# Attention before a dense layer: q, k and v laid out by head pair on the host, the first batch alone, the second wholly between dense steps, weight tiles in 4 KB rows

## The chip, the cores and the metric

The kernel runs on one core of one Trainium2 chip. The metric is the time of one execution in device microseconds (us). One execution of the kernel before was taken with the hardware profiler; its rows stand below.

## The reference

Two batches, 8 heads, 576 positions, head dimension 64, fp32. Attention is the sum of two parts; then follow a dense mixture of 4 experts (every expert for every token) and a routed one of 8 experts (one expert for a token).

```python
q_d, k_d, v_d = (a.reshape(B, H, 144, 4, D).mean(axis=3) for a in (q, k, v))
out_up = np.repeat(softmax(q_d @ k_d.T / 8) @ v_d, 4, axis=2)
mask = np.abs(pos[:, None] - pos[None, :]) < 4
out_local = softmax(np.where(mask, q @ k.T / 8, -1e9)) @ v
x = (out_up + out_local).transpose(0, 2, 1, 3).reshape(1152, 512)
p = domain_probs / domain_probs.sum(-1)
x = sum(p[:, e:e+1] * (relu(x @ w1[e]) @ w2[e]) for e in range(4))
# then: cosine logits with 8 expert embeddings, best expert of each token, its gate * (relu(x @ w1b[e]) @ w2b[e])
```

## The kernel before

Attention works on 8 units; a unit is one pair of heads of one batch, its 2 x 64 dimensions on the 128 partitions. Units 0 to 3 are the first batch, 4 to 7 the second. For each unit q and k are loaded with positions on the partitions (`load_rows`, in runs of 256 bytes), transposed on TensorE (`turn`, `turn_k`, `turn_q`), copied out of PSUM (`keep_k`, `keep_q`) and pooled by fours (`pool_k`, `pool_q`, on POOL, GpSimd). v is loaded twice: by groups of four rows (`load_vg`) for the pooled part and by nine windows of 72 rows (`load_vw`) for the local part. Scores of the nine local blocks (`scores_a`, `scores_b`) and of the pooled part (`scores_d`) go to PSUM with the mask added by a matmul, then come maxima, exponentials, sums, scaling, transposes of P (`turn_pa`, `turn_pb`, `turn_pd`), copies out of PSUM (`keep_*`), products with v (`value_*`), the sum of both parts (`add_*`) and a split of x into a high and a low part (`hi`, `lo`), since the dense matmuls run as three products of such parts.

The order of all this is written out by hand. `ROUND` lists the 39 stages; in round i the stage with lag l works on unit i − l, so that up to six units are in flight. Every engine and every DMA queue runs its instructions in the order in which they are issued, and an instruction that waits holds up all behind it on its engine; all plain loads are issued on SP's queue. The attention runs alone until 36 pieces past the stage `lo` of unit 3. The 55 pieces left of 312 are then issued between the first 24 of 32 steps of the dense layer (line 582 on). A pair of steps is one `first_half` (12 matmuls of 256 columns) and one `second_half` (6 of 512 columns, of the pair before); 16 pairs cover the first two token chunks, that is 512 tokens of the first batch. The third chunk needs the second batch.

`Weights` loads tiles of 128 x 1024 fp32 (512 KB) into four raw tiles, splits each in two halves of a high and a low part (`halves`), and hands the raw tile back to load the next (`load_to`). A tile of w1 is loaded in runs of 1 KB, one of w2 in runs of 2 KB. When the second half of a tile is split, it loads ahead as far as raw tiles are there:

```python
if s == 1:
    self.raw.append(self.raws.pop(i))
    self.split += 1
    self.load_to(self.split + self.ahead)
```

Of the kernel before, what the change touches and what calls it, by code (L numbers as in the profile page):

```python
# [29 lines left out]
class Attention:  # L30
# [4 lines left out]
    ROUND = [  # L35
        ("value_a", 4), ("value_b", 4), ("value_d", 4), ("pool_v", 3), ("keep_q", 2), ("scores_a", 2), ("exp_b", 3),
        ("pool_k", 2), ("max_d", 3), ("sum_l", 3), ("scores_b", 2), ("lo", 5), ("max_a", 2), ("keep_d", 4),
        ("exp_d", 3), ("load_q", 1), ("pool_q", 2), ("exp_a", 2), ("scale_a", 3), ("scale_b", 3), ("sum_d", 3),
        ("scores_d", 2), ("turn_pa", 3), ("keep_pa", 3), ("load_vw", 2), ("scale_d", 3), ("add_a", 4), ("turn_pb", 3),
        ("add_b", 4), ("hi", 4), ("turn_pd", 3), ("turn_k", 1), ("turn_q", 1), ("load_k", 0), ("load_vg", 1),  # L40
        ("keep_pb", 3), ("keep_k", 1), ("keep_pd", 3), ("max_b", 2),
# [24 lines left out]
    def load_k(self, u, d):  # L66
        d["kn"] = self.load_rows(u, self.k, "kn")

    def load_q(self, u, d):
        d["qn"] = self.load_rows(u, self.q, "qn")  # L70

    def load_rows(self, u, src, tag):
        b, hp = self.units[u]
        t = self.ld.tile([96, 6, 2, D], F32, tag=tag, name=tag, bufs=2)
        for h in range(2):
            self.nc.sync.dma_start(out=t[:, :, h, :], in_=src[b, 2 * hp + h].rearrange("(j r) d -> j r d", r=6))
        return t

    def load_vg(self, u, d):
        nc, ld = self.nc, self.ld  # L80
        b, hp = self.units[u]
        vg = ld.tile([72, 2, 2, 4 * D], F32, tag="vg", name="vg", bufs=2)
        for h in range(2):
            nc.sync.dma_start(
                out=vg[:, :, h, :], in_=self.v[b, 2 * hp + h].rearrange("(a j r) d -> j a (r d)", a=2, r=4)
            )
        d["vg"] = vg

    def load_vw(self, u, d):
        nc, ld = self.nc, self.ld  # L90
        b, hp = self.units[u]
        vw = ld.tile([72, 9, 2, D], F32, tag="vw", name="vw", bufs=2)
        for h in range(2):
            off = ((b * H + 2 * hp + h) * S + 60) * D
            nc.sync.dma_start(
                out=vw[:, 1:8, h, :],
                in_=bass.AP(tensor=self.v.tensor, offset=off, ap=[[D, 72], [64 * D, 7], [1, D]]),
            )
        vs = self.v[b, 2 * hp:2 * hp + 2]
        nc.sync.dma_start(out=vw[0:68, 0], in_=vs[:, 0:68, :].rearrange("h p d -> p h d"))  # L100
        nc.sync.dma_start(out=vw[0:68, 8], in_=vs[:, 508:576, :].rearrange("h p d -> p h d"))
        d["vw"] = vw

    def turn(self, src, spots):
        ident = self.cst["ident"]
        for r, (t, o) in enumerate(spots):
            self.nc.tensor.transpose(t[:, o:o + 96], src[:, r].rearrange("p h d -> p (h d)"), ident[0:96, 0:96])

    def turn_k(self, u, d):
        d["tk"] = self.bank(), self.bank()  # L110
        self.turn(d["kn"], [(d["tk"][0], 96 * r) for r in range(5)] + [(d["tk"][1], 0)])

    def turn_q(self, u, d):
        d["tq"] = self.bank()
        self.turn(d["qn"], [(d["tk"][1], 96 + 96 * r) for r in range(4)] + [(d["tq"], 96 * r) for r in range(2)])

    def spread(self, T, t, o, r0, r1):
        src = t[:, o:o + 96 * (r1 - r0)].rearrange("p (r j) -> p r j", j=96)
        return T.rearrange("p (j r) -> p r j", r=6)[:, r0:r1, :], src

    def keep_k(self, u, d):
        kT = self.wk.tile([128, S], F32, tag="kT", name="kT", bufs=1)
        for t, o, r0, r1, e in ((d["tk"][0], 0, 0, 5, "a"), (d["tk"][1], 0, 5, 6, "a")):
            self.copy(e, *self.spread(kT, t, o, r0, r1))
        d["kT"] = kT

    def keep_q(self, u, d):
        qT = self.wk.tile([128, S], F32, tag="qT", name="qT", bufs=1)
        for t, o, r0, r1, e in ((d["tk"][1], 96, 0, 4, "a"), (d["tq"], 0, 4, 6, "v")):
            dst, src = self.spread(qT, t, o, r0, r1)  # L130
            if e == "a":
                self.nc.scalar.activation(out=dst, in_=src, func=AF.Copy, scale=0.125)
            else:
                self.nc.vector.tensor_scalar(out=dst, in0=src, scalar1=0.125, scalar2=None, op0=ALU.mult)
        d["qT"] = qT

    def fours(self, engine, T, out):

        e = self.nc.gpsimd if engine == "p" else self.nc.vector
        Tv = T.rearrange("p (g r) -> p g r", r=4)  # L140
        t = self.wk.tile([128, 144, 2], F32, tag="pt", name="pt")
        e.tensor_tensor(t, Tv[:, :, 0:2], Tv[:, :, 2:4], op=ALU.add)
        e.tensor_tensor(out, t[:, :, 0], t[:, :, 1], op=ALU.add)

    def pool_k(self, u, d):
        d["kd"] = self.cst["kd"][u % 2]
        self.fours("p", d["kT"], d["kd"][:, 0:144])

    def pool_q(self, u, d):
        d["qd"] = self.cst["qd"][u % 2]  # L150
        self.fours("p", d["qT"], d["qd"][:, 0:144])

    def pool_v(self, u, d):
        vg = d["vg"]
        e = self.nc.gpsimd if "p" == "p" else self.nc.vector
        t = self.wk.tile([72, 2, 2, 128], F32, tag="pv", name="pv")
        e.tensor_tensor(t, vg[:, :, :, 0:128], vg[:, :, :, 128:256], op=ALU.add)
        vd = self.wk.tile([72, 2, 2, D], F32, tag="vd", name="vd", bufs=2)
        e.tensor_tensor(vd, t[:, :, :, 0:64], t[:, :, :, 64:128], op=ALU.add)
        d["vd"] = vd  # L160
# [20 lines left out]
    def scores_a(self, u, d):  # L181
        self.scores(d, 0, 5)

    def scores_b(self, u, d):
        self.scores(d, 5, 9)
# [11 lines left out]

    def max_a(self, u, d):
        d["mx"] = self.wk.tile([128, 9], F32, tag="mx", name="mx", bufs=2)
        self.nc.vector.tensor_reduce(out=d["mx"][:, 0:5], in_=d["s0"], axis=AX.X, op=ALU.max, negate=True)  # L200

    def max_b(self, u, d):
        self.nc.vector.tensor_reduce(out=d["mx"][:, 5:9], in_=d["s5"], axis=AX.X, op=ALU.max, negate=True)

    def max_d(self, u, d):
        m = self.wk.tile([128, 3], F32, tag="mxd", name="mxd", bufs=2)
        self.nc.vector.tensor_reduce(out=m, in_=d["sd"], axis=AX.X, op=ALU.max, negate=True)
        self.nc.vector.tensor_scalar(out=m, in0=m, scalar1=1.0 / 16, scalar2=None, op0=ALU.mult)
        d["mxd"] = m

    def exp(self, P, src, bias, sm, scale=1.0):
# [4 lines left out]
    def exp_a(self, u, d):  # L216
        d["P"] = self.wk.tile([128, 9, 72], F32, tag="P", name="P", bufs=2)
        d["sm"] = self.wk.tile([128, 9], F32, tag="sm", name="sm", bufs=2)
        for i in range(5):
            sm = d["sm"][:, i:i + 1] if i < 5 else None  # L220
            self.exp(d["P"][:, i], d["s0"][:, i], d["mx"][:, i:i + 1], sm)

    def exp_b(self, u, d):
        for i in range(5, 9):
            sm = d["sm"][:, i:i + 1] if i < 5 else None
            self.exp(d["P"][:, i], d["s5"][:, i - 5], d["mx"][:, i:i + 1], sm)

    def exp_d(self, u, d):
        d["Pd"] = self.wk.tile([128, 3, 144], F32, tag="Pd", name="Pd", bufs=2)
        d["smd"] = self.wk.tile([128, 3], F32, tag="smd", name="smd", bufs=2)  # L230
        for i in range(3):
            sm = d["smd"][:, i:i + 1] if i < 3 else None
            self.exp(d["Pd"][:, i], d["sd"][:, i], d["mxd"][:, i:i + 1], sm, 1.0 / 16)

    def weights(self, P, sm, known, weight):

        if known < sm.shape[1]:
            self.nc.vector.tensor_reduce(out=sm[:, known:], in_=P[:, known:], axis=AX.X, op=ALU.add)
        self.nc.vector.tensor_scalar(out=sm, in0=sm, scalar1=1e-9, scalar2=weight, op0=ALU.add, op1=ALU.mult)
        self.nc.vector.reciprocal(sm, sm)  # L240
        return sm

    def sum_l(self, u, d):
        d["rc"] = self.weights(d["P"], d["sm"], 5, 1.0)

    def sum_d(self, u, d):
        d["rcd"] = self.weights(d["Pd"], d["smd"], 3, 4.0)

    def scale(self, engine, P, rc):
        e = self.nc.gpsimd if engine == "p" else self.nc.vector  # L250
        e.tensor_tensor(P, P, rc.unsqueeze(2).to_broadcast(list(P.shape)), op=ALU.mult)

    def scale_a(self, u, d):
        self.scale("p", d["P"][:, 0:4], d["rc"][:, 0:4])
# [1034 lines left out]
```

## Time and profile before

| | us |
|---|---|
| median of 3 runs (lowest, highest) | 696.08 (694.25, 696.15) |
| the profiled execution, its own time | 692.35 |
| its span, first to last instruction | 690.6 |
| TensorE (PE) busy | 653.1 (95%) |
| VectorE (DVE), ScalarE (ACT), GpSimd (POOL) busy | 345.9, 261.0, 144.6 |
| mean granted TensorE clock | 0.989 |

Times in rows are us from the first instruction; PEld is the weight load of TensorE, which overlaps its matmuls. "Idle before" names what ended an engine's idle time. The granted clock is a share of the full 2.4 GHz.

### The profile page before, as it was taken

The numbers are of one execution on the slowest core, as the hardware profiler recorded it, in microseconds if no ns is written. First come the engines' busy times: TensorE is split into PE (matmuls) and PEld (weight loads), VectorE is DVE, ScalarE is ACT, GpSimd is POOL, SyncE is SP. The second block draws the span as 40 slices with busy tenths as digits, with TensorE's granted clock in tenths as the row PEclk, the third lists the DMA queues.
The fourth block names the chain that finished last, engine by engine and source line by source line (L and its number), as shares of the span: only waits on it lengthen the run. The fifth ranks groups of instructions, "written<-read, shape, count | busy, mean of one in ns | idle before, by whom it ended". The sixth has DMA issues, their size and how long they took to land. (4 is left out here: it accounts for less than half of the span.)

```text
span 690.6 us, 11440 instructions
## 1 busy us (share of the span) xinstructions
PE 653.1 (95%) x4287; PEld 578.2 (84%) x4287; DVE 345.9 (50%) x825; ACT 261.0 (38%) x653; POOL 144.6 (21%) x203
## 2 busy tenths in 40 slices
PE   5798999999999999999999999999799998999896
PEld 4677899989999999999999999999698877788675
DVE  2667764213444122342132326989662269489751
ACT  3577742112232111231111222243342367488642
POOL 4678511100000000000000001748441122121111
PEclk9799999999999999999999999999999999999999
DMA  8866250000331002031001126251672166499600
GB/s 219 207 146 147 57 162 3 1 1 31 93 121 62 1 0 62 1 125 58 1 30 62 54 68 187 62 184 64 181 240 78 32 211 204 151 333 349 222 20 29
DMA packets 78364, 73.57 MB, mean 107 GB/s; under 512 B 32286, under 2 KB 62254, under 8 KB 78272
## 3 DMA queue, kind: packets, MB, share of 16 engines
q1 hardware_dynamic: 75968, 66.09, 31.6%
q0 software_dynamic: 2304, 6.33, 3.1%
q8 instruction: 48, 0.79, 0.5%
q14 instruction: 44, 0.36, 0.2%
HBM read 66.10 MB, written 7.09 MB: 106 GB/s over the span
## 5 line engine op out<-in xcount | busy, mean ns | idle before, releaser
L529 PE MATMUL psb<-wh,hT 128*128 128x512 f32 x576 | 197.6, 395 | 0.0
L520 DVE SCALAR_TENSOR_TENSOR hT<-psb,hT 128x384 fp32r<-128x384 f32 (+1 forms) x104 | 54.7, 526 | 221.2 <-ACT hT L519 221.1
L519 ACT ACTIVATE hT<-psb 128x384 fp32r<-128x384 f32 (+1 forms) x104 | 48.6, 467 | 290.2 <-PE psb L515 290.1
L515 PE MATMUL psb<-xh,wh 128*128 128x384 f32 (+1 forms) x416 | 135.5, 326 | 0.0
L515 PE MATMUL psb<-xl,wh 128*128 128x384 f32 (+1 forms) x416 | 134.9, 324 | 0.0
L515 PE MATMUL psb<-xh,wl 128*128 128x384 f32 (+1 forms) x416 | 134.9, 324 | 0.0
L529 PEld LDWEIGHTS psb<-wh,hT 128*128 128x128 f32 x576 | 108.6, 189 | 20.6 <-issue 0.4
L529 PE MATMUL psb<-wl,hT 128*128 128x512 f32 x288 | 113.4, 394 | 0.0
L403 POOL TENSOR_TENSOR wl<-raw,wh 128x512 fp32r<-128x512 f32 x24 | 31.8, 1358 | 306.2 <-DVE waste L752 290.4
L515 PEld LDWEIGHTS psb<-xh,wh 128*128 128x128 f32 x416 | 78.2, 188 | 4.3
L515 PEld LDWEIGHTS psb<-xl,wh 128*128 128x128 f32 x416 | 78.3, 188 | 4.1
L515 PEld LDWEIGHTS psb<-xh,wl 128*128 128x128 f32 x416 | 78.2, 188 | 0.0
L403 DVE TENSOR_TENSOR wl<-raw,wh 128x512 fp32r<-128x512 f32 x108 | 71.9, 712 | 4.5 <-ACT wh L399 3.7
L399 ACT CAST wh<-raw 128x512 fp32r<-128x512 f32 x126 | 70.8, 624 | 0.1
L529 PEld LDWEIGHTS psb<-wl,hT 128*128 128x128 f32 x288 | 54.3, 189 | 7.8
L1064 PE MATMUL psb<-wh,gx 128*128 128x256 f32 x288 | 58.2, 289 | 0.1
L1032 PE MATMUL psb<-wh,hT 128*128 128x512 f32 x160 | 54.2, 399 | 1.6 <-ACT sqd L1042 0.8
L1064 PEld LDWEIGHTS psb<-wh,gx 128*128 128x128 f32 x288 | 46.2, 189 | 1.9 <-issue 1.2
L1032 PEld LDWEIGHTS psb<-wh,hT 128*128 128x128 f32 x160 | 30.1, 188 | 7.8 <-ACT sqd L1042 1.2
L1064 PE MATMUL psb<-wl,gx 128*128 128x256 f32 x144 | 35.9, 283 | 0.0
L1032 PE MATMUL psb<-wl,hT 128*128 128x512 f32 x80 | 31.5, 394 | 0.0
L1064 PEld LDWEIGHTS psb<-wl,gx 128*128 128x128 f32 x144 | 27.2, 189 | 0.4
(250 smaller groups left out, 849.8 us busy)
## 6 DMA issues: line engine op xcount, KB each, us to landing
raw<-in_moe_w_dram SPq DMA_DIRECT2D x66, 512.0 KB
late_raw<-in_moe_w_dram SPq DMA_DIRECT2D x20, 512.0 KB
acc<-in_moe_w_dram SPq DMA_DIRECT2D x10, 512.0 KB
kn<-in_k_dram SPq DMA_DIRECT2D x16, 144.0 KB
qn<-in_q_dram SPq DMA_DIRECT2D x16, 144.0 KB
vg<-in_v_dram SPq DMA_DIRECT2D x16, 144.0 KB
rows<-acc SPq DMA_DIRECT2D x9, 256.0 KB
vw<-in_v_dram SPq DMA_DIRECT2D x16, 126.0 KB
```

The costliest lines, as they stand in the source:

```text
L399: nc.scalar.copy(hi[:, c], t[:, c])
L403: lo_eng.tensor_tensor(lo[:, c], t[:, c], hi[:, c].bitcast(F32), op=ALU.subtract)
L515: nc.tensor.matmul(t, a[:, kk, fs], b_[:, kk, xs], start=(n == 0), stop=(n == 11))
L519: nc.scalar.activation(out=hi, in_=t, func=AF.Relu)
L520: nc.vector.scalar_tensor_tensor(out=lo, in0=t, scalar=0.0, in1=hi.bitcast(F32), op0=ALU.max, op1=ALU.subtract)
L529: nc.tensor.matmul(ys[t], a[:, ts], b_[:, f % 2, :], start=(f == 0 and j == 0), stop=(f == 7 and j == 2))
L1032: nc.tensor.matmul(y, gh[:, f, a], b_[:, f % 2, :], start=(n == 0), stop=(n == 23))
L1064: nc.tensor.matmul(dst, a[:, kk], w[:, kk, :], start=(n == 0), stop=(n == 11))
```

## The change

The host lays out q and k as they are needed on chip, one array of 128 partitions (two heads x 64 dimensions) x 576 positions for a unit, and v as 72 rows that hold the nine windows (1152 numbers) and the groups of four (1024 numbers) of two heads. The transposes of q and k and the copies behind them go away, and with them the factor 0.125 on q; it is now in the exponentials' scale and in a scaling of the maxima (`top`). A unit has four loads instead of ten. q is pooled on DVE by one reduce, k on POOL as before. The local blocks are parted 4 and 5, not 5 and 4; two copies (`od`, half of `dT`) move from DVE to ACT; sums are inverted in two parts (`sum_a`, `sum_b`). The weights are stored so that each tile is one array of 128 rows of 4 KB. `run` takes an order and a range of units: `ALONE` for the first batch, with one weight half after each `exp_b`, `BESIDE` for the second, its 144 pieces spread over the first 28 of the 32 dense steps. No stage of the second batch is issued ahead of the first dense step.

```diff
+    ALONE = [
+        ("load_qk", 0), ("max_a", 1), ("sum_a", 2), ("scale_a", 2), ("value_d", 4), ("keep_d", 4), ("pool_v", 2),
+        ("turn_pa", 3), ("exp_d", 2), ("sum_b", 2), ("turn_pd", 3), ("value_b", 4), ("scores_a", 0), ("sum_d", 2),
+        ("add_a", 4), ("turn_pb", 3), ("add_b", 4), ("keep_pa", 3), ("keep_db", 3), ("pool_q", 0), ("pool_k", 0),
+        ("scores_b", 0), ("exp_a", 1), ("keep_8", 3), ("value_a", 3), ("scale_b", 2), ("keep_da", 3), ("scale_d", 2),
+        ("max_b", 1), ("max_d", 1), ("hi", 4), ("keep_pb", 3), ("scores_d", 0), ("lo", 4), ("exp_b", 1), ("load_v", 1),
+    ]
+    BESIDE = [
+        ("keep_pb", 4), ("scores_b", 2), ("max_b", 2), ("pool_k", 1), ("scores_a", 1), ("pool_v", 3), ("exp_a", 2),
+        ("sum_a", 2), ("exp_b", 2), ("scores_d", 2), ("max_d", 2), ("value_a", 4), ("value_d", 4), ("sum_b", 2),
+        ("load_v", 2), ("keep_d", 4), ("turn_pa", 3), ("value_b", 4), ("exp_d", 2), ("add_a", 4), ("keep_pa", 3),
+        ("scale_d", 3), ("turn_pd", 3), ("keep_da", 3), ("add_b", 4), ("load_qk", 0), ("scale_a", 2), ("keep_db", 3),
+        ("sum_d", 2), ("keep_8", 3), ("hi", 4), ("scale_b", 2), ("pool_q", 1), ("lo", 4), ("turn_pb", 3), ("max_a", 1),
+    ]
...
+    def run(self, order, units):
+        for i in range(len(units) + max(lag for _, lag in order)):
+            for name, lag in order:
+                if 0 <= i - lag < len(units):
+                    u = units[i - lag]
                     getattr(self, name)(u, self.st.setdefault(u, {}))
                     yield name, u
...
+    def load_qk(self, u, d):
+        b, hp = self.units[u]
+        t = self.ld.tile([128, 2, S], F32, tag="qk", name="qk", bufs=3)
+        self.nc.sync.dma_start(out=t[:, 1, :], in_=self.k[b, hp])
+        self.nc.sync.dma_start(out=t[:, 0, :], in_=self.q[b, hp])
+        d["qT"], d["kT"] = t[:, 0, :], t[:, 1, :]
+    def load_v(self, u, d):
         b, hp = self.units[u]
+        vg = self.ld.tile([72, 2, 2, 4 * D], F32, tag="vg", name="vg", bufs=2)
+        self.nc.sync.dma_start(out=vg.rearrange("p a h d -> p (a h d)"), in_=self.v[b, hp, :, 1152:])
+        vw = self.ld.tile([72, 9, 2, D], F32, tag="vw", name="vw", bufs=3)
+        self.nc.sync.dma_start(out=vw.rearrange("p i h d -> p (i h d)"), in_=self.v[b, hp, :, 0:1152])
+        d["vg"], d["vw"] = vg, vw
...
     def pool_q(self, u, d):
         d["qd"] = self.cst["qd"][u % 2]
-        self.fours("p", d["qT"], d["qd"][:, 0:144])
+        self.nc.vector.tensor_reduce(
+            out=d["qd"][:, 0:144], in_=d["qT"].rearrange("p (g r) -> p g r", r=4), axis=AX.X, op=ALU.add
+        )
...
+    def top(self, m, s, scale):
+        self.nc.vector.tensor_reduce(out=m, in_=s, axis=AX.X, op=ALU.max)
+        self.nc.vector.tensor_scalar(out=m, in0=m, scalar1=-scale, scalar2=None, op0=ALU.mult)
...
+            self.nc.sync.dma_start(out=t, in_=w[c])
...
+        half = H // 2
+        for name, u in att.run(att.ALONE, range(half)):
+            if name == "load_v" and u < 2:
+                W.load_to(u + 1)
+            elif name == "load_v" and u == 3:
                 W.load_to(NRAW)
+            elif name == "exp_b":
+                W.halves(1, "a", "v")
...
-        W.halves(max(0, 4 - W.half), "v", "v")
-        rest, done = pieces - first, 0
+        run = att.run(att.BESIDE, range(half, 2 * half))
+        rest, done = half * len(att.BESIDE), 0
         for step in range(32):
...
-            while done < min(rest, -(-rest * (step + 1) // 24)):
+            while done < min(rest, -(-rest * (step + 1) // 28)):
                 next(run)
                 done += 1
             if W.half < 2 * n_a:
```

## Rows read from the trace of the kernel before

**Rows 1.** Busy us of each engine in a stretch; then granted clock, DMA share, GB/s.

```profile
49.09:57.65 8.56, 7.58 (x124) 6.10 (x122) 6.82 (x17) 6.69 (x29) 6.84 (x10) 1.00 0.60 145
...
80.00:100.00 20.00, 20.00 (x170) 17.79 (x169) 13.81 (x28) 11.30 (x35) 3.95 (x3) 1.00 0.62 175
```

**Rows 2.** Timeline of PE: start us, us, line, output<-inputs, shape, count.

```profile
5.05 1.19 PE L107 MATMUL psb<-ident,kn 96*128 96x96 f32 x6 [5.05 <-DMA kn<-in_k_dram]
...
27.84 2.19 PE L319 MATMUL psb<-acc,vw 68*64 68x64 f32 x36
...
38.80 1.27 PE L319 MATMUL psb<-acc,vw 68*64 68x64 f32 x36
...
75.81 0.39 PE L515 MATMUL psb<-xh,wh 128*128 128x256 f32 x1
...
98.35 0.40 PE L529 MATMUL psb<-wh,hT 128*128 128x512 f32 x1
...
101.13 0.39 PE L529 MATMUL psb<-wh,hT 128*128 128x512 f32 x1
...
128.41 0.34 PE L515 MATMUL psb<-xh,wh 128*128 128x384 f32 x1
```

**Rows 3.** Timeline of PE: a steady round's scores; values of a unit beside dense.

```profile
49.09 0.32 PE L165 MATMUL psb<-mask,dup 64*128 64x360 bf16 x1
...
50.12 0.29 PE L165 MATMUL psb<-mask,dup 64*128 64x288 bf16 x1
...
50.89 0.90 PE L192 MATMUL psb<-kd,qd 64*64 64x144 f32 x12
...
93.69 1.27 PE L319 MATMUL psb<-acc,vw 68*64 68x64 f32 x36
...
95.43 0.50 PE L529 MATMUL psb<-wh,hT 128*128 128x512 f32 x1
```

**Rows 4.** Groups of 0 to 80 us: busy us, mean ns | idle before.

```profile
L403 DVE TENSOR_TENSOR wl<-raw,wh 128x512 fp32r<-128x512 f32 x5 | 4.6, 921 | 0.1
...
L200 DVE TENSOR_REDUCE mx<-psb 128x5 f32<-128x360 f32 x8 | 4.2, 523 | 3.9 <-PE psb L175 3.9
...
L134 DVE TENSOR_SCALAR qT<-psb 128x192 f32<-128x192 f32 x8 | 4.0, 504 | 11.0 <-PE psb L107 11.0
...
L64 DVE COPY dT<-psb 72x288 f32<-72x288 f32 x6 | 2.7, 450 | 0.2
...
L208 DVE TENSOR_SCALAR mxd<-mxd 128x3 f32<-128x3 f32 x7 | 2.6, 366 | 0.2
...
L64 DVE COPY od<-psb 128x144 f32<-128x144 f32 x6 | 1.8, 300 | 0.0
...
L240 DVE RECIPROCAL sm<-sm 128x9 f32<-128x9 f32 x7 | 1.5, 216 | 0.2
```

**Rows 5.** Two stretches of 2 us, columns as in rows 1.

```profile
4.00:6.00 2.00, 0.95 (x6) 0.93 (x6) 0.00 (x0) 0.00 (x0) 0.00 (x0) 1.00 0.92 158
12.00:14.00 2.00, 2.00 (x26) 1.72 (x22) 0.55 (x2) 1.51 (x10) 1.52 (x2) 1.00 1.06 360
```

**Rows 6.** Timeline around a q load: SP's issues and PE's wait.

```profile
20.23 0.39 SPq L375 DMA_DIRECT2D raw<-in_moe_w_dram  x1
...
20.72 1.25 SPq L76 DMA_DIRECT2D qn<-in_q_dram  x2
...
26.69 1.22 PE L107 MATMUL psb<-ident,qn 96*128 96x96 f32 x6 [1.83 <-DMA qn<-in_q_dram]
```

**Rows 7.** The last part, columns as in rows 1.

```profile
610.00:650.00 40.00, 35.29 (x229) 30.79 (x228) 34.08 (x69) 31.05 (x65) 6.08 (x6) 1.00 0.98 327
```

**Rows 8.** Stretches around a fall and rise of PE's clock, columns as in rows 1.

```profile
20.00:26.00 6.00, 3.09 (x28) 2.11 (x23) 5.43 (x11) 3.42 (x15) 4.87 (x5) 1.00 0.81 209
28.00:36.00 8.00, 8.00 (x96) 6.47 (x97) 3.85 (x12) 4.35 (x22) 5.53 (x8) 0.50 1.01 233
38.00:40.00 2.00, 2.00 (x49) 1.89 (x49) 1.75 (x6) 1.61 (x4) 0.33 (x1) 1.00 0.66 148
```

More of the change, by code (lines that the diff above doesn't have):

```diff
@@ L79, in load_vg @@
-    def load_vg(self, u, d):
-        nc, ld = self.nc, self.ld
-        b, hp = self.units[u]
[L82 to L135, printed above, removed]
@@ L231, in exp_d, with inverse, sum_a, sum_b @@
         for i in range(3):
[L232 to L238, printed above, removed]
+            self.exp(d["Pd"][:, i], d["sd"][:, i], d["mxd"][:, i:i + 1], d["smd"][:, i:i + 1], 0.125 / 16)
+    def inverse(self, sm, weight):
         self.nc.vector.tensor_scalar(out=sm, in0=sm, scalar1=1e-9, scalar2=weight, op0=ALU.add, op1=ALU.mult)
         self.nc.vector.reciprocal(sm, sm)
-        return sm
-    def sum_l(self, u, d):
-        d["rc"] = self.weights(d["P"], d["sm"], 5, 1.0)
+    def sum_a(self, u, d):
+        self.inverse(d["sm"][:, 0:4], 1.0)
+    def sum_b(self, u, d):
+        self.nc.vector.tensor_reduce(out=d["sm"][:, 4:9], in_=d["P"][:, 4:9], axis=AX.X, op=ALU.add)
+        self.inverse(d["sm"][:, 4:9], 1.0)
     def sum_d(self, u, d):
[L247 to L251, printed above, removed]
+        self.inverse(d["smd"], 4.0)
+    def scale(self, P, rc):
+        self.nc.gpsimd.tensor_tensor(P, P, rc.unsqueeze(2).to_broadcast(list(P.shape)), op=ALU.mult)
     def scale_a(self, u, d):
-        self.scale("p", d["P"][:, 0:4], d["rc"][:, 0:4])
+        self.scale(d["P"][:, 0:4], d["sm"][:, 0:4])
     def scale_b(self, u, d):
-        self.scale("p", d["P"][:, 4:9], d["rc"][:, 4:9])
+        self.scale(d["P"][:, 4:9], d["sm"][:, 4:9])
     def scale_d(self, u, d):
-        self.scale("p", d["Pd"], d["rcd"])
+        self.scale(d["Pd"], d["smd"])
     def turn_p(self, d, t, o, i):
@@ L324, in value_a @@
     def value_a(self, u, d):
-        self.values(d, 0, 5)
+        self.values(d, 0, 4)
     def value_b(self, u, d):
-        self.values(d, 5, 9)
+        self.values(d, 4, 9)
     def add(self, d, b0, b1):
         n = 64 * (b1 - b0)
+        if "x" not in d:
+            d["x"] = self.wk.tile([128, S], F32, tag="x", name="x")
         self.nc.vector.tensor_tensor(
@@ L563 @@
         nc.gpsimd.dma_start(out=pr, in_=probs.rearrange("(t p) e -> p t e", p=128))
-        pieces = len(att.units) * len(att.ROUND)
-        run = att.run()
-        first = 0
-        for n, (name, u) in enumerate(run, 1):
-            if n == 14:
-                W.load_to(NRAW)
-            if n >= 20 and (n - 20) % 8 == 0 and W.half < 4:
-                W.halves(1, "v", "v")
-            if name == "lo" and u == H // 2 - 1:
-                first = n + 36
-            if n == first:
-                break
+        half = H // 2
[3 more added lines that the diff above has]
+            elif name == "load_v" and u == 3:
+                W.load_to(NRAW)
+            elif name == "exp_b":
+                W.halves(1, "a", "v")
         nc.vector.tensor_reduce(out=psm, in_=pr, axis=AX.X, op=ALU.add)
@@ L1261, with laid @@
 _OUTS = [((N, DM), "float32")]
+def laid(np, name, a):
+    if name in ("q", "k"):
+        return a.reshape(B, H // 2, 2, S, D).transpose(0, 1, 2, 4, 3).reshape(B, H // 2, 128, S)
+    if name == "v":
+        w = np.zeros((B, H // 2, 72, 9, 2, D), a.dtype)
+        for i in range(9):
+            c0, c1 = max(64 * i - 4, 0), min(64 * i + 68, S)
+            w[:, :, 0:c1 - c0, i] = a[:, :, c0:c1].reshape(B, H // 2, 2, c1 - c0, D).transpose(0, 1, 3, 2, 4)
+        g = a.reshape(B, H // 2, 2, 2, 72, 4 * D).transpose(0, 1, 4, 3, 2, 5)
+        return np.concatenate([w.reshape(B, H // 2, 72, -1), g.reshape(B, H // 2, 72, -1)], axis=3)
+    if name.endswith("_w1"):
+        return a.reshape(-1, 4, 128, 4, 256).transpose(0, 3, 2, 1, 4).reshape(-1, 4, 128, 1024)
+    if name.endswith("_w2"):
+        return a.reshape(-1, 4, 2, 128, DM).transpose(0, 1, 3, 2, 4).reshape(-1, 4, 128, 1024)
+    return a
 def kernel(**inputs):
```

104 lines of the change are left out of this document (34 added, 70 removed).

## Prediction, made before the result was known

> **What bounds the kernel now.** I read the page's totals first, then the busy time by stretch, the matrix unit's timeline, the groups of instructions of the first 80 us, and last the load queue. By stretch there are two regimes [rows 1]. From 80 us on TensorE (PE) is full, with no idle time left in 80 to 100, so every microsecond of PE work added or removed there counts whole. Before 80 us no engine is full: in a steady round of the attention (one unit, that is one head pair of one batch, passes each stage once) PE has 7.58 of 8.56 us, DVE 6.82, ACT 6.69 and POOL 6.84. The first dense matmul starts at 75.81, and its third token chunk, the first that needs the second batch, at 128.41 [rows 2]. What comes behind 128.41 is the same work in both kernels. So the forecast is a sum of two terms: how much earlier dense work starts, and how much more attention PE then carries between dense steps.
>
> **Dense side: what attention costs there.** A pair of dense steps (one call of each half) takes 101.13 − 98.35 = 2.78 us [rows 2]. Ahead of 128.41 stand 16 first halves and 15 second ones, 15.5 pairs, 43.1 us. The stretch took 128.41 − 75.81 = 52.6, so attention took 9.5 us of PE between the steps. That was the score blocks 5 to 8 and the pooled scores of the last unit, and all transposes of P and value products of the last two (55 pieces of the hand-written order were left). Scores of one unit, from a steady round: 50.89 − 49.09 = 1.80 us for the local blocks and 0.90 for the pooled ones, 2.7; the part named is 50.89 − 50.12 + 0.90 = 1.67 [rows 3]. So turns and values cost (9.5 − 1.67) / 2 = 3.9 us a unit, seams with the dense work included; directly, the values alone are 95.43 − 93.69 = 1.74 [rows 3]. After the change four whole units lie there: 4 × (2.7 + 3.9 + 0.2 for more seams) = 27.2 us, which is 17.7 more. The PSUM banks get tighter: at the change of chunk four are held for dense sums, and a unit's pieces want up to six. The trace has no row for such a wait; below it costs nothing (DVE is busy 13.81 and ACT 11.30 of 20 us in 80 to 100, with attention and weight halves beside the dense work, so they can keep up [rows 1]), above perhaps one dense pair, 2.8. I take 1.1, nearer to the covered end. Together +18.8.
>
> **Alone side: when dense starts.** Gone per unit are 12 transposes of q and k on PE, three copies out of PSUM on ACT, one on DVE and the two POOL adds that pool q; of loads, ten strided issues become four. DVE becomes the busiest engine: 6.82 a unit now, less 0.50 (q), 0.45 (half of dT) and 0.30 (od), which go or move to ACT, plus a reduce of q over 576 elements (0.52 for 360, so about 0.8), four more operations on a few columns (two scalings behind the maxima, a second addition and reciprocal of the sums; 0.22 for a reciprocal now, 0.37 for a scaling, 0.8 in all, as most are like the first) and one low half of a weight tile (0.92) [rows 4]: 8.1 us. Four units are 32.4. The first score block can start where the first transposes do now, 5.05 us [rows 2], and takes about 1.5; the last unit's copies, products and adds that DVE waits for are some 3. Nothing else waiting, dense starts at 5.05 + 1.5 + 32.4 + 3 = 42 us. That is the lower end.
>
> Two waits speak against it. They come from the order of SP's queue. Every second weight half frees a raw tile and at once loads ahead as far as there are tiles: four weight tiles, the last of which has to wait until DVE has split the first one, the last DVE instruction of round 2. Behind that waiting load on SP stand v of unit 1 and q, k of unit 3. DVE gets there at about 5.05 + 1.5 + 10 us of work and some gaps, say 18. Then 0.52 + 0.63 + 0.59 MB have to move: at the best rate of the trace, 360 GB/s [rows 5], 4.9 us, plus issue and flight. Now a q load issued at 20.72, right behind such a weight load, is used at 26.69, and PE idles for it [rows 6]. So q, k of unit 3 are there at about 25, while PE has done its 3 units of scores and unit 0's first turns by 19.5: it waits 5.5 us, with unit 0's other turns and values queued behind, and DVE's pooling of q with two maxima behind it. The second: the next reload waits for DVE's end of round 4, v of unit 3 stands behind it, and POOL's sum of v stands ahead of the two scalings that the last turns need. 0.82 MB are 2.3 us, about 2 of flight, less about 1 that POOL has left to do: 3.5 us. With 1 us for a low clock I take 42 + 5.5 + 3.5 + 1 = 52 us. The upper end is the last rival's.
>
> The rule behind these waits is in the Trainium skill, "DMA: Bandwidth & Descriptors", section "Anatomy of one DMA": DMA engines do not wait on semaphores, the issuing sequencer does, before dispatch. By that rule everything behind the reload is late as above, and the start is 52; were it not so, it would be 42. The row agrees so far as a load behind a reload was late there.
>
> **Sum.** −(75.8 − 52) + 18.8 = −5.0 us. The profiled execution took 692.35 (span 690.6 and 1.75 around it), so it would be 687.3 like for like; the median of the runs shown, 696.08, lies 3.7 above that execution, and the forecast for it is **691.1 us**.
>
> **Weights in 4 KB rows.** The loads were 1 KB or 2 KB runs. In the dense part nobody waits for weights, so I cost them at nothing there; the cover is PE's full queue. In 610 to 650 the DMA share is near 1, and DVE, which splits, is busy 34.1 of 40 us [rows 7]. No wait there is put down to a weight load.
>
> **Rivals.**
> *The loads do not hold (23%).* The reload is ready earlier than I place it, or the large rows move faster; for it speaks that rows of 2.3 to 4.6 KB replace runs of 256 bytes, which held the DMA at share 0.92 with only 158 GB/s [rows 5]. Dense starts at 42: −33.8 + 18.8 = −15.0, 681.1 us.
>
> *The clock stays low (30%), the one on the other side.* PE's granted clock was 1.00 in 20 to 26, where PE was busy 3.1 of 6 us, then 0.50 in 28 to 36, where it was full, and 1.00 again from 38 [rows 8]. In that stretch a round (values of one unit to those of the next) took 38.80 − 27.84 = 10.96 instead of 8.56 [rows 1, 2]. The waits above leave PE as idle as there, and the drain of four units has no fifth to fill it; two units of the pipeline hardly overlap. If each of four rounds costs the 2.4 us more, the start goes from 52 to 61.6: −14.2 + 18.8 = +4.6, 700.7 us. It decides from a dense start later than 75.8 − 18.8 = 57. Against it: the first dense work is dense enough to raise the clock again. The Trainium skill, "TensorE: Matmul & The Clock Gate", Part 1, has the throttled state as the default, released by activity; by it the alone stage with less PE work for the same latency is the place to lose the clock, and the time goes towards 700.7. The rows just named agree.
>
> *The rows pay in the tail (5%).* If what looks like DVE's pace in 610 to 650 were hidden load time, its 5.9 idle us could go: 691.1 − 5.9 = 685.2. Against it: no wait on these tiles is listed.
>
> **Numbers.** Forecast 42%, then 23, 30 and 5. A measurement of this kernel tells about 0.3%, 2.1 us, from no change: faster is under 694.0, slower over 698.2. Of the 42, 32 lie under 694.0 (a start up to 55 us) and 10 within; of the clock's 30, 23 lie over 698.2 and 7 within. Faster 0.32 + 0.23 + 0.05 = 0.60, same 0.17, slower 0.23. The forecast's own range is 686 to 696 (start 47 to 57); for 8 in 10 it reaches to the loads that hold nothing up, 679, and to the low clock, 700.
>
> **What would show it.** The first dense matmul at about 52 us; third chunk some 71 us later (43.1 + 27.2 + 1.1). PE idle before the scores of unit 3 with a load of q or k as releaser, and before the last turns of P with POOL as releaser, itself held by v. Granted clock 0.50 somewhere in 20 to 52. No transposes from q and k, no ACT copies of them. Behind the third chunk the same length as before. Wrong would be: a start at 42 without those waits; PE idle between the dense steps for banks or for DVE by more than 3 us; a tail that changes.

## The result, and the profile after

The changed kernel took **705.23 us** (median of 4 runs, 703.41 to 706.0), the kernel before 695.5 in the same comparison (694.25 to 696.15): ratio 1.0139, 95% interval 1.0121 to 1.0157. It is slower, and 14.1 us over the forecast of 691.1, outside the range of 679 to 700. The profiled execution took 703.41 with a span of 701.7.

The timeline of the matrix unit in the changed kernel, for the rows of [rows 2] that start the dense work and its third chunk:

```profile
58.23 0.58 PE L462 MATMUL psb<-xh,wh 128*128 128x256 f32 x1
...
136.15 0.34 PE L462 MATMUL psb<-xh,wh 128*128 128x384 f32 x1
```

Dense work starts 17.58 us earlier than before (75.81), but the third chunk comes 77.92 us behind it, where it was 52.60: 25.32 more. So at the third chunk the kernel is 7.74 us behind. From there to the end of the span it needs 565.6 us, against 562.2 before: another 3.4 us.

Busy time by stretch, of the stage before dense work and of the stretch from the first dense matmul to the third chunk (columns as in [rows 1]):

```profile
20.00:58.00 38.00, 22.81 (x274) 17.42 (x274) 18.66 (x49) 14.88 (x60) 15.58 (x21) 0.69 0.42 123
...
58.23:136.15 77.92, 74.97 (x720) 63.76 (x719) 44.92 (x115) 35.61 (x129) 22.74 (x32) 0.95 0.30 89
```

In the 38 us before dense work no engine is busy for more than 23: this stage is made of waits. Which ones, the view of waits up to 150 us says (total us, times, longest):

```profile
PE psb L122 <- DMA qk<-in_q_dram: 14.5, 5, 8.5
...
POOL pv L104 <- DMA vg<-in_v_dram: 11.8, 3, 4.7
...
PE psb L211 <- POOL P L198: 3.4, 1, 3.4
...
PE psb L260 <- ACT dT L68: 2.8, 2, 1.5
```

PE waits for q, and POOL for v, and PE for POOL. Why q and v are late is in the load queue's timeline (SP; the second number is the time from the first of the grouped issues to the end of the last):

```profile
5.58 13.40 SPq L330 DMA_DIRECT2D raw<-in_moe_w_dram  x4
19.03 0.40 SPq L82 DMA_DIRECT2D vg<-in_v_dram  x1
...
19.95 0.35 SPq L75 DMA_DIRECT2D qk<-in_k_dram  x1
20.35 0.58 SPq L76 DMA_DIRECT2D qk<-in_q_dram  x1
...
41.86 0.35 SPq L330 DMA_DIRECT2D raw<-in_moe_w_dram  x1
42.32 0.33 SPq L82 DMA_DIRECT2D vg<-in_v_dram  x1
```

Four weight loads stand in a row, and the last of them holds the queue until 18.98; of the 13.40 us the view of waits puts 8.4 on DVE's split of the first tile. v of unit 1 and k, q of unit 3 are issued right behind it. The same happens at 41.86, with v of unit 3 behind the reload; between 21.79 and 41.86 SP issues nothing. On PE and POOL the answers are these rows, in order of time:

```profile
14.56 0.71 PE L122 MATMUL psb<-qk 64*64 64x68 f32 x16 [1.98 <-DMA qk<-in_q_dram]
...
27.75 1.21 PE L122 MATMUL psb<-qk 64*64 64x68 f32 x16 [8.54 <-DMA qk<-in_q_dram]
...
44.87 1.23 PE L260 MATMUL psb<-dT,vd 72*64 72x144 f32 x8 [1.49 <-ACT dT L68]
...
50.55 0.42 PE L211 MATMUL psb<-ident,P 128*68 128x128 f32 x1 [3.44 <-POOL P L198]
```

```profile
47.69 1.26 POOL L104 TENSOR_TENSOR pv<-vg 72x512 f32<-72x512 f32 x1 [4.73 <-DMA vg<-in_v_dram]
```

POOL's sum of v stands ahead of the second scaling of P, and so a late v holds the last turns of P. A last view of the changed kernel: the granted clock in two stretches, 0.50 in both (the second reaches into the first dense steps).

```profile
22.00:30.00 8.00, 2.25 (x21) 1.65 (x21) 2.20 (x6) 0.00 (x0) 4.68 (x6) 0.50 0.78 211
46.00:60.00 14.00, 10.12 (x89) 8.12 (x88) 4.08 (x9) 3.23 (x8) 5.72 (x8) 0.50 0.36 108
```

The theory tested first: the mechanism is the one forecast (loads behind a waiting weight reload), with larger sums on both sides. Its rivals: the low clock is the cost; the 4 KB rows harm; the new order loses even with its loads in time.

### The profile page after: what moved, and what is told of

Read it like the earlier page. It is cut to its first block, busy times and chain, and to the rows that moved or that the text cites. A ratio compares the mean times of both kernels' runs of the same rounds, so it can differ in the third digit from the quotient of the medians.

```text
span 701.7 us, 11167 instructions
## 1 busy us (share of the span) xinstructions
PE 654.9 (93%) x4191; PEld 576.0 (82%) x4191; DVE 345.5 (49%) x837; ACT 253.9 (36%) x641; POOL 134.0 (19%) x187
## 5 line engine op out<-in xcount | busy, mean ns | idle before, releaser
L462 PE MATMUL psb<-xh,wh 128*128 128x384 f32 (+1 forms) x416 | 137.1, 329 | 0.0
L346 ACT CAST wh<-raw 128x512 fp32r<-128x512 f32 x130 | 73.4, 624 | 0.0
L350 DVE TENSOR_TENSOR wl<-raw,wh 128x512 fp32r<-128x512 f32 x108 | 69.7, 690 | 7.0 <-ACT wh L346 6.2
```

What stands on the lines that cost most here:

```text
L346: nc.scalar.copy(hi[:, c], t[:, c])
L350: lo_eng.tensor_tensor(lo[:, c], t[:, c], hi[:, c].bitcast(F32), op=ALU.subtract)
L462: nc.tensor.matmul(t, a[:, kk, fs], b_[:, kk, xs], start=(n == 0), stop=(n == 11))
```

## Experiments

A table first. "Start" is the first dense matmul and "third" the first one of 384 columns, both from PE's timeline of the run; "beside" is third minus start. All dense work ahead of the third chunk is 43.1 us, so third minus 43.1 is what all attention and its waits cost up to there, alone and beside. "Tail" is from the third chunk to the end of the span.

| kernel | start | third | beside | third − 43.1 | tail | time | ratio to before (95%) |
|---|---|---|---|---|---|---|---|
| before | 75.81 | 128.41 | 52.6 | 85.3 | 562.2 | 695.5 | 1 |
| changed | 58.23 | 136.15 | 77.9 | 93.1 | 565.6 | 705.23 | 1.0139 (1.0121 to 1.0157) |
| e1: three ahead, alone stage | 51.95 | 130.18 | 78.2 | 87.1 | 566.3 | 697.45 | 1.004 (1.001 to 1.0071) |
| e2: three ahead, both | 51.77 | 125.23 | 73.5 | 82.1 | 567.1 | 693.93 | 1.0001 (0.9965 to 1.0037) |
| f3: one ahead, then three | 47.50 | 120.37 | 72.9 | 77.3 | 563.5 | 689.11 | 0.9938 (0.9905 to 0.9971) |
| g3: none until v of unit 3 | 39.12 | 115.81 | 76.7 | 72.7 | 569.9 | 686.01 | 0.9849 (0.9795 to 0.9904) |
| h1: g3, 10 pieces moved up | 49.61 | 119.74 | 70.1 | 76.6 | 567.6 | 684.72 | 0.9839 (0.9798 to 0.9879) |
| f1: changed, PE kept busy | 57.37 | 134.97 | 77.6 | 91.9 | 567.1 | 703.27 | 1.0132 (1.0078 to 1.0185) |
| e3: before, 4 KB weight rows | 76.38 | 128.96 | 52.6 | 85.9 | 561.8 | 693.4 | 0.9987 (0.996 to 1.0014) |
| e4: before, q, k, v laid out | 64.51 | 117.09 | 52.6 | 74.0 | 564.5 | 683.27 | 0.9856 (0.9804 to 0.9909) |
| f2: e4 and 4 KB rows | 65.93 | 118.53 | 52.6 | 75.4 | 565.9 | 685.87 | 0.9891 (0.983 to 0.9952) |
| g1: f2, one tile ahead | 67.11 | 119.71 | 52.6 | 76.6 | 565.8 | 686.42 | 0.9877 (0.9828 to 0.9926) |
| g2: g1, engines moved | 68.15 | 120.74 | 52.6 | 77.6 | 567.0 | 687.11 | 0.9879 (0.985 to 0.9908) |
| f4: f2, cut a round early | 62.70 | 125.76 | 63.1 | 82.7 | 565.6 | 690.08 | 0.9946 (0.9924 to 0.9969) |

Start, third and tail are of one profiled execution each (h1's is the longest of its six); the time is the median of the timed runs, and each ratio is to runs of the kernel before made beside them.

**e1: fewer weight tiles ahead, alone stage only.** The waiting reload is to be taken out of the queue by loading one tile less ahead: the next tile goes into one that was freed a tile earlier.

```
+        W.ahead = NRAW - 1
         half = H // 2
         for name, u in att.run(att.ALONE, range(half)):
...
+        W.ahead = NRAW
         run = att.run(att.BESIDE, range(half, 2 * half))
```

> One line: while the first batch runs alone, the weight loader runs one tile less ahead, so that a reload goes to a raw tile that was freed one tile earlier and does not wait on SP. Theory (order of the loads): the changed kernel's PE waits of 8.5 us for q of unit 3 and 3.4 us behind v of unit 3 go, and with them the low clock that follows; first dense matmul at 45 to 50 us instead of 58.2, time about 9 to 11 us under the changed kernel, that is about that of the kernel before (ratio 0.997 to 1.003). Rival (clock): PE is idle in the alone stage anyway and stays at half rate; start at 54 or later, at most 4 us won, ratio 1.008 or more. Rival (dense side): the loss is made between the dense steps and the start does not reach the end.

Start 51.95, 6.28 us earlier, which is later than the 45 to 50 expected; beside stays at 78.2. The total of PE's waits for q went from 14.5 to 9.9 us, the longest from 8.5 to 3.7. The queue's order is a cause, and not all of it: now q of unit 3 is issued at 13.06, with no reload that waits for DVE ahead of it, and PE still waits for it.

**e2: the same beside the first 32 dense steps too.**

```
+        W.ahead = NRAW - 1
         half = H // 2
...
+    W.ahead = NRAW
     if stage == 1:
```

> The same for the dense steps with the second batch too, restored behind them. Theory (order of the loads): on top of the run with the alone stage only, the waits of 2.2 and 0.8 us for q of later units and the half clock at 76 to 79 us go: third chunk 71 to 73 us behind the first dense matmul instead of 77.9, 3 to 5 us under the other, ratio to before 0.990 to 0.996. Rival (banks): PE idle stays between dense steps with other releasers than a load; the stretch stays at 76 or more.

Beside fell to 73.5, near the 71 to 73 expected, and PE has no idle time left there (73.46 busy of 73.46). The time, 1.0001, is outside the 0.990 to 0.996 expected; the tail of this execution is 4.9 us longer than before. In the alone stage the longest wait left is for q of unit 3 (e1, the same program up to there, had 3.67 in its profile):

```profile
25.34 1.21 PE L122 MATMUL psb<-qk 64*64 64x68 f32 x16 [5.09 <-DMA qk<-in_q_dram]
...
51.77 0.58 PE L462 MATMUL psb<-xh,wh 128*128 128x256 f32 x1
```

```profile
51.77:125.23 73.46, 73.46 (x720) 62.43 (x719) 44.37 (x115) 35.69 (x129) 24.07 (x32) 0.97 0.23 71
```

**e3: the rows of the weights alone**, on the kernel before: the weights' part of `laid` and this in `load_to`:

```
-            if which == 0:
...
+            self.nc.sync.dma_start(out=t, in_=w[c])
```

> The kernel before with the weight tiles in rows of 4 KB and nothing else changed. Theory: no engine waits for a weight tile, ratio 0.997 to 1.003, first dense matmul within 1.5 us of 75.8. Rival (rows pay): the tail from 600 us on gets 3 to 6 us shorter, ratio 0.991 to 0.996. Rival (rows cost): the loss of 9.7 us is partly theirs, ratio over 1.003.

0.9987 (0.996 to 1.0014): no measurable effect, neither gain nor harm. The tail is 561.8 against 562.2.

**e4: the layout of q, k, v alone**, in the order of the kernel before: the new `load_qk` and `load_v` bodies, no turns and copies of q and k, the scale 0.125 in the exponent; pooling stays on POOL.

```
     ROUND = [
-        ... ("keep_q", 2), ("load_q", 1), ("turn_k", 1), ("turn_q", 1), ("keep_k", 1) ...
```

> The kernel before with q, k and v from the host's layout: no transposes of q and k and no copies of them, its order of stages and its cut ahead of the dense steps kept, weights in their old rows. Theory: the layout is a gain by itself and the new order loses it; a round goes from 8.56 to 7 or 7.5 us (POOL 6.84 and DVE about 6.7 are the most loaded), first dense matmul at 62 to 67, 9 to 13 us under before, ratio 0.981 to 0.987. Rival: the round is held by the chain of POOL's scalings and the turns of P and stays at 8.3 or more; only the start gains, 2 to 4 us, ratio 0.994 to 0.997.

Ratio 0.9856: the layout is a gain of 1.4%, and the third chunk comes 11.32 us earlier than before, with beside unchanged at 52.6. A steady round became this one (columns as in [rows 1]):

```profile
48.28:55.88 7.60, 6.72 (x111) 5.10 (x109) 6.62 (x18) 5.13 (x26) 6.91 (x10) 1.00 0.34 88
```

7.60 us in place of 8.56, with PE at 6.72 and POOL at 6.91: two engines near full. The gain of the change is here; the rest of it, the new order with its loads above all (f2 and g2 below bear on the rows and the engine moves), gives it back and costs 1.4% beyond that.

**f1: PE kept busy through the waits.** Products of constants into the bank that the next real products overwrite; nothing reads them.

```
+    def busy(self, t, n):
+        for _ in range(n):
+            self.nc.tensor.matmul(
+                t[:, 0:360], self.cst["dup"], self.cst["mask"][:, 0:5, :],
+                start=True, stop=True, skip_group_check=True,
+            )
```

> The changed kernel with idle-time work for PE: small bf16 products of constants, written into the bank that the next products fill, ahead of the scores of units 2 and 3 (10 and 48 of them), of the last turns of unit 3 (20) and of the pooled values of units 1 and 2 (6 and 8); nothing reads them. Theory that the low clock is a cost of its own on top of the waits: granted clock 1.00 through 20 to 58; PE's 23 us of work in 20 to 58 shrink by 4 to 6, and the first dense matmul, 58.23, comes at 53 to 55; third chunk 3 to 6 us earlier, ratio to before 1.006. Rival, the low clock only fills time in which PE would wait for loads, DVE or POOL anyway: start within 1 us of 58.2 and ratio 1.013 as the changed kernel.

```profile
20.00:50.00 30.00, 27.10 (x287) 18.04 (x285) 16.33 (x45) 13.82 (x58) 13.20 (x17) 1.00 0.54 154
50.00:60.00 10.00, 9.46 (x86) 8.29 (x86) 4.27 (x10) 2.31 (x5) 2.63 (x5) 0.52 0.03 11
```

The clock is 1.00 from 20 to 50, where it was 0.50 in 22 to 30 and from 46 on, and the start moves by only 0.86 us, as the rival had it. So in the first of these stretches the low clock cost little: the work that it stretched had to wait for loads anyway. The second stretch was not tested by this run, since behind two short waits for POOL (1.02 and 0.56) the clock fell again. There it does cost: from the last turns of P to the first dense matmul the changed kernel takes 58.23 − 51.41 = 6.82 us, this run 57.37 − 50.55 = 6.82, and g3, which does the same work at clock 1.00, 39.12 − 35.12 = 4.00. That is 2.8 us.

**f2: all layouts in the old order**, e4 with the 4 KB rows of e3.

> Host layouts of q, k, v and of the weights (4 KB rows), in the order of the kernel before: the change without its new order. If the new order is the whole loss: 683 us like the layout alone (ratio 0.986), start 64.5, third chunk 117. If the 4 KB rows by themselves do something once q, k and v no longer crowd the queues: third chunk or tail moves by more than 1 us against the layout alone, up or down.

0.9891, with e4's 0.9856 inside its interval: the two cannot be told apart. The third chunk is 1.44 us later than in e4, behind a wait for pooled q of 4.6 us where e4 had 2.98; one profile of each does not say that the rows are the reason.

**f3: one tile ahead in the alone stage, three beside.**

```
+        W.ahead = 1
         half = H // 2
...
+        W.ahead = NRAW - 1
         run = att.run(att.BESIDE, range(half, 2 * half))
```

> The changed kernel with one weight tile loaded ahead in the alone stage (in place of four) and three beside the first 32 dense steps. With three ahead the scores of unit 3 still waited 5.1 us for q, behind three weight tiles and v on a full queue. Theory that the loads' order and volume is the wait: q of unit 3 in time, that wait under 1.5 us, start at 47 to 49, ratio to before 0.992 to 0.996. Rival, loads of q, k, v alone fill the queue, or DVE and ACT take over as the wait: start at 50 to 52, ratio 1.000.

```profile
47.50:120.37 72.87, 72.25 (x721) 61.03 (x719) 44.58 (x116) 35.62 (x129) 24.12 (x32) 1.00 0.23 72
```

Start 47.50, ratio 0.9938: as the theory said for the time, though two waits for q of 2.56 and 2.54 were left, where it wanted under 1.5. This row is also the clean price of attention beside dense steps: clock 1.00, PE busy 72.25 of which 43.1 is dense, so 29.2 us for four units.

**f4: the old order, cut one round earlier.**

```
             if name == "lo" and u == H // 2 - 1:
-                first = n + 31
+                first = n
```

> As f2, but dense steps begin as soon as the first batch is done, some 31 pieces (one round, 7.6 us) earlier; these pieces go between dense steps. Theory that a unit costs as much beside dense steps as in a steady round alone, since PE has 6.7 of 7.6 us in such a round: start near 57, third chunk near 116 to 117, ratio 0.984 to 0.987, the same as f2. Rival, work beside dense steps is free because other engines hide: third chunk at 110, ratio 0.976. Rival, it costs more there (the new order's loss is in the dense side): third chunk 119 to 121.

0.9946, with a median 4.2 us above f2's, though the two intervals overlap. Beside grew by 63.06 − 52.60 = 10.46 us for the 31 pieces. Alone, in f2, they take 65.93 − 59.19 = 6.74, with PE busy for 5.86 of it (on PE they are a round without `scores_b`):

```profile
59.19 0.95 PE L138 MATMUL psb<-kd,qd 64*64 64x144 f32 x12
...
65.93 0.39 PE L454 MATMUL psb<-xh,wh 128*128 128x256 f32 x1
```

The stretch beside in f4:

```profile
62.70:125.76 63.06, 59.88 (x524) 51.24 (x522) 35.50 (x87) 25.80 (x87) 17.59 (x25) 1.00 0.22 67
```

PE's own work in the stretch rose by 59.88 − 52.60 = 7.28, 1.4 more than alone; the other 3.2 us are idle time, most of it for the DVE halves of hT and for POOL. So the last rival holds: the pieces cost 3.7 us more beside dense steps. The alone stage of this execution, with the same instructions, was also 3.5 us later than f2's (62.70 against 59.19, with a wait for pooled q of 3.04 at 39.31 that f2 did not have), so beside says more here than the third chunk does.

**g1: old order, all layouts, one tile ahead.**

```
+        W.ahead = 1
         pieces = len(att.units) * len(att.ROUND)
...
             if n == 8:
-                W.load_to(NRAW)
+                W.load_to(1)
```

> All host layouts in the order of the kernel before, with one weight tile loaded ahead until dense steps begin (in place of four). If weight tiles in the first 20 us hold up k, q and v here too: the waits for pooled q (4.6 us, once) and the DMA share of 0.95 in 10 to 20 go, start 61 to 63 in place of 65.9, ratio 0.981 to 0.984. Rival, the attention's own loads fill the queue: start 65 to 66, ratio 0.989.

The rival held: start 67.11, ratio 0.9877, as f2. The DMA share in 10 to 20 is 0.99. In the old order the loads ahead are no cost that shows.

**g2: g1 with the change's engine moves** (`pool_q` as a DVE reduce; `od` and both halves of `dT` by ACT).

> As g1, with the engine moves of the change: pooling of q as one DVE reduce, pooled output and both halves of dT copied by ACT. A steady round of the old order with host layouts is 7.60 us with POOL busy 6.91, PE 6.72, DVE 6.62, ACT 5.13. If POOL sets the round: POOL falls by 1.1, DVE stays near 6.6, ACT rises to 5.9, and the round goes to 6.9 to 7.1, PE's own work; start 57 to 60, ratio 0.975 to 0.980. Rival, the reduce costs DVE more than it saves POOL: round 7.6 or longer, no change against g1.

No gain. A round of it is 7.95 us, longer than 7.60, although no engine is near full:

```profile
32.65:40.60 7.95, 6.35 (x111) 5.27 (x110) 6.22 (x18) 5.76 (x28) 5.68 (x7) 1.00 0.55 167
...
36.22 0.95 PE L140 MATMUL psb<-kd,qd 64*64 64x144 f32 x12 [1.60 <-DVE smd L189]
```

With POOL relieved (5.68 for 6.91), a wait for DVE has taken its place: PE stands 1.05 to 1.60 us in each round at the pooled scores. Their pooled q is now made on DVE: its reduce starts at 35.33, right behind the low part of x (34.08) and the maxima (34.69). The row names the sum of Pd (`smd`), which DVE runs next.

**g3: no weights until v of unit 3 is issued.**

```
-            if name == "load_v" and u < 2:
-                W.load_to(u + 1)
-            elif name == "load_v" and u == 3:
+            if name == "load_v" and u == 3:
                 W.load_to(NRAW)
-            elif name == "exp_b":
-                W.halves(1, "a", "v")
+            elif name == "lo" and u > 0:
+                W.halves(u // 3 + 1, "a", "v")
```

> The changed kernel with no weight tile loaded until v of unit 3 is issued (and the four weight halves of the alone stage after unit 1's end); three ahead beside dense steps. With one tile ahead PE still waited 2.6 us each for q of units 2 and 3. If the weights in the queue are what is left: both waits under 0.7 us, start 44 to 45.5. Rival, the queue is full of the attention's own 0.9 MB a unit: waits as they are, start 47 to 48; or the weight halves, now late, hold up the dense start: first matmul waits for the split, 48 or later. Ratio to before by the first 0.990, by the others 0.994 or more.

The start, 39.12, is better than either side expected, and q of unit 3 does not wait at all (its scores at 19.24 follow the mask at once, where the changed kernel had 8.54). But q of unit 2 waits 2.18, where under 0.7 was expected, and no weight is in the queue then. So that wait is of the attention's own loads (1.2 MB a unit, not 0.9), as the rival had it.

```profile
13.67 0.71 PE L122 MATMUL psb<-qk 64*64 64x68 f32 x16 [2.18 <-DMA qk<-in_q_dram]
...
19.24 0.71 PE L122 MATMUL psb<-qk 64*64 64x68 f32 x16
...
39.12 0.39 PE L462 MATMUL psb<-xh,wh 128*128 128x256 f32 x1
```

```profile
39.12:50.00 10.88, 9.42 (x82) 7.43 (x79) 7.94 (x19) 4.42 (x14) 0.48 (x1) 0.69 0.64 174
```

The third chunk gains less, beside being 76.7: 1.46 us of waits for x of unit 3, and behind them a clock of 0.50 from 44 to 48. The tail takes 7.7 us more than before (below). Ratio 0.9849, level with e4.

**h1: g3 with the first pieces of the second batch ahead of dense work.**

```
-        rest, done = half * len(att.BESIDE), 0
+        rest, done = half * len(att.BESIDE), 10
+        for _ in range(done):
+            next(run)
```

> The changed kernel with no weights until v of unit 3, plus the first 10 pieces of the second batch (both local score groups of unit 4 and one of unit 5, some 2.5 us of PE work) put ahead of the first dense step; beside dense steps the share of pieces stays as it was. In the run before PE waited 1.05 and 0.41 us inside the first dense group for x of unit 3, and its clock was 0.50 from 43 to 49. If those waits are what lets the clock fall: no wait, clock 1.00 through 40 to 60, third chunk 4 to 5 us earlier, 111 to 112, ratio 0.977 to 0.981. Rival, the clock falls anyway, with the early idle time of the drain: third chunk 114 to 116, ratio 0.984 to 0.986. What the tail does with its clock adds some 3 us either way in one profile.

Inconclusive for what it was to tell. The six timed runs lie between 678.13 and 689.01, and the profile is of the longest, whose clock was low from before the first dense step on:

```profile
36.00:52.00 16.00, 16.00 (x153) 13.07 (x152) 9.90 (x22) 5.59 (x13) 2.74 (x5) 0.50 0.49 172
```

Whether the waits for x set off the fall of the clock in g3 stays open. By the ratio, 0.9839, h1 and g3 cannot be told apart, nor either from e4.

## Why the prediction was wrong, by its own steps

Like for like it put the profiled execution at 687.3; it took 703.41. The 16.1 us between lie in three places: the start (58.23, not 52: 6.2), beside (77.92, not 71.4: 6.5), and the tail (3.4, forecast as nothing).

**Two waits of the load queue: right in kind, too small in sum.** This is the step that failed first. The weight reload held SP to 18.98 (forecast 18), v of unit 1 and k, q of unit 3 were issued behind it, and PE was ready for q at 19.2 (forecast 19.5). The rule cited from the Trainium skill ("DMA: Bandwidth & Descriptors", "Anatomy of one DMA": the issuing sequencer waits, not the DMA engine) agrees with the row of 13.40 us. While SP was held, the DMA share fell, to 0.38 in 16 to 18:

```profile
16.00:18.00 2.00, 1.77 (x27) 1.32 (x23) 1.34 (x4) 1.84 (x8) 1.95 (x3) 1.00 0.38 147
...
20.00:28.00 8.00, 0.24 (x4) 0.25 (x6) 0.99 (x5) 0.00 (x0) 3.70 (x6) 0.56 0.85 252
```

But the wait for q was 8.54, not 5.5. The release came 1.0 later than forecast, PE was ready 0.3 earlier, and from the release to q's first use at 27.75 passed 8.8 us instead of 7. The mis-sized term is that transfer: it was priced at the best rate of the trace, 360 GB/s, and the row shows 252; v of unit 2, issued at 21.03 right behind q, was moved in the same stretch and is not in the sum. g3, without weights, has no wait for q of unit 3; e1, f3 and e2 lie between with 3.7, 2.5 and 5.1. A wait for q of unit 2, 1.98, was not foreseen and is of another kind: that q was issued before the reload, and g3 has 2.18 there without any weights. The second wait, for v through POOL, was forecast at 3.5 (its terms, 2.3 + 2 − 1, make 3.3) and measured at 3.44 on PE; on POOL itself it was 4.73, so that the two numbers agree is in part luck. The row of before that this step leaned on ([rows 6]) shows a q load that comes late behind a weight load, not a reload that waits: no wait of SP is listed for it.

**The base of 42 us: too high.** From its first scores on (4.50), PE waited 1.98 and 8.54 us for q, 1.28 and 1.49 for dT behind ACT (not in the forecast; e1, e2 and f3 have 2.9 to 3.4 of it, and no run takes it out), 3.44 for POOL, and four times under 0.5, together 18.0. That and 2.8 for the clock (below) leave 58.2 − 18.0 − 2.8 = 37.4: the start is 37.4 + 18.0 + 2.8, where the forecast was 42 + 9 + 1. g3, with 3.5 us of waits in its 39.12, bears a base under 42 out. Of the base's terms, DVE had 30.21 us of work up to the start where the sum has 32.4 (though its 0.8 for four small operations is 1.2 by its own rows), and the first scores began at 4.50 and not at 5.05; the rest of the 4.6 is not told apart. The base was too high and the waits too low, and so the errors partly cancelled.

**1 us for a low clock: 2.8.** It was there in the place named (0.50 somewhere in 20 to 52). The rival "the clock stays low" is not what happened, though the time came out above it: it priced each of four rounds at 2.4 us, and f1, with the clock held at 1.00 up to 50, starts 0.86 us earlier. Most of its cost is in the stretch after the last wait, 6.82 us for 4.00; f1's 0.86 is inside the 37.4 above.

**Dense side: the work nearly right, the waits for loads put at nothing.** This is the second step that failed. Forecast 71.4, of it 27.2 for attention and 1.1 for banks. f3 has PE busy 72.25 at full clock for the same work, so attention is 29.2, and no wait for a bank is listed; together 0.85 over. The changed kernel has 74.97, 2.7 more, as its clock was 0.50 to 62 and again after a wait at 74.78; and 2.95 us of idle time, waits for q of units 6 and 7 (2.19 and 0.76). These q loads stand on SP behind reloads that could be issued only at 65.98 and 83.77, when DVE had split a tile (the longest such wait of SP is 19.8 us), and PE is ready for them 5.0 and 3.5 us after their issue:

```profile
65.98 0.33 SPq L330 DMA_DIRECT2D raw<-in_moe_w_dram  x1
...
67.62 0.44 SPq L76 DMA_DIRECT2D qk<-in_q_dram  x1
```

```profile
74.78 0.72 PE L122 MATMUL psb<-qk 64*64 64x68 f32 x16 [2.19 <-DMA qk<-in_q_dram]
```

0.85 + 2.7 + 2.95 = 6.5. The prediction had put both of its load waits into the alone stage, and asked of the dense side only whether banks or engines keep up. The same queue runs through both, and the same `load_to` stands ahead of q there. e2, which mends that alone, issues q of unit 6 at 41.72, has neither wait, and took beside from 78.2 to 73.5.

**Weights in 4 KB rows at nothing: right** (e3).

**The decision point, a start later than 57, was set too late.** 58.23 was later than that, so it decided rightly here, but it rests on the 18.8 of the dense side. With the price measured beside (25.3) the point is 75.8 − 25.3 = 50.5, and e1, at 51.95, is just behind it (1.004). e2, with 73.5 beside, decides at 54.9; it is 3.2 us ahead at the third chunk, and its tail, 4.9 longer, takes that back (1.0001).

**Why the new order has little to win even with its loads in time.** Attention beside dense steps costs PE its full 29.2 us for four units, 7.3 a unit, and a steady round alone costs 7.60, with PE 6.72 of it (e4). There is little idle time of PE in a round to be hidden behind dense work; only the fill and the drain of the pipeline are. f4 shows it on the old order: pieces that take 6.74 alone cost 7.28 of PE and 3.2 of new waits beside dense steps. So the best of the new order (g3, third − 43.1 of 72.7) only just passes the layout in the old order (e4, 74.0), and by the time the two cannot be told apart. If f3's beside could follow g3's start, the third chunk would come at 39.1 + 72.9 = 112.0, 5 us ahead of e4: an estimate from two runs, and no run has both.

**What stays open: the tail.** It was forecast as the same length, and its 3.4 us are the third part of the miss. The part behind the third chunk has the same instructions, and took 1.3 to 7.7 us longer in every kernel with q, k, v laid out, in either order, and no longer in e3. Each is one execution, and the kernel before alone ran from 690.8 to 698.79 us in the 25 beside e1 to e4, so the smaller of these differences may be no more than that. In the changed kernel 3.1 of the 3.4 us are lost in the last 27. The output writes of the last two experts on POOL's timeline, in the changed kernel:

```profile
684.75 1.01 POOL L979 DMA_INDIRECT out_dram<-sqd,oidx  x1 [6.42 <-ACT sqd L985]
696.86 1.00 POOL L979 DMA_INDIRECT out_dram<-sqd,oidx  x1 [11.10 <-ACT sqd L985]
```

In the kernel before:

```profile
674.50 1.01 POOL L1036 DMA_INDIRECT out_dram<-sqd,oidx  x1 [4.20 <-DVE oidx L1043]
685.76 1.00 POOL L1036 DMA_INDIRECT out_dram<-sqd,oidx  x1 [10.25 <-ACT sqd L1042]
```

The lag is 8.02 us one write earlier (675.25 against 667.23), 10.25 at the first of these and 11.10 at the second. In between the changed kernel's clock falls behind a pause of PE, and in g3 the same:

```profile
674.00:680.00 6.00, 3.33 (x20) 2.65 (x20) 5.05 (x12) 4.43 (x10) 1.92 (x2) 0.98 0.13 37
680.00:684.00 4.00, 4.00 (x14) 3.15 (x13) 1.74 (x4) 0.58 (x2) 0.00 (x0) 0.60 0.10 26
```

```profile
656.00:662.00 6.00, 2.89 (x15) 1.87 (x14) 4.69 (x10) 3.40 (x9) 2.23 (x2) 0.84 0.04 9
662.00:668.00 6.00, 6.00 (x22) 5.00 (x21) 2.77 (x6) 1.53 (x4) 0.00 (x0) 0.59 0.16 46
```

The kernel before has the pause too, less deep (PE busy 2.88 of 4 us in 666 to 670), and its profiled execution kept 1.00 behind it. No run changed the tail by itself, so why it holds there is not shown.

## What to carry to other kernels

In a queue that issues in order, a load that has to wait for a buffer delays every load behind it by its whole wait: go through the issue order of each stage, the later ones too, and ask of each prefetch which urgent load stands behind it. Prefetch no further than free buffers go, and not before the loads that the next wait hangs on; here that moved the start from 58.2 to 39.1 us with the same work (g3). Look first whether loads are what the stage waits for: in the old order, one tile ahead in place of four showed nothing (g1). And before interleaving one stage with another to "fill" it, compare the bound engine's busy time a round with the round's length: at 6.72 of 7.60 there is little to fill.

## What was not expected of the hardware

- A low granted clock cost little here where a wait followed and in full where work followed: keeping PE busy changed the clock in 20 to 50 from as low as 0.50 to 1.00 and the start by 0.86 us, while the stretch of work behind the last wait took 6.82 us at 0.50 and 4.00 at 1.00.
- h1's times spread more than those of before: 678.13 to 689.01 in 6 runs, against 690.3 to 696.47 in 11 beside them. Why is not shown.
- Transfers in rows of 4 KB in place of 1 and 2 KB did nothing for the time that could be measured, 0.9987, though packets fell from 78364 to 53788 (e3).
